# Splitting the first x loads into partition halves and the first gate steps into tiles, in an SSM and gated-MLP kernel

## The chip, the cores and the metric

The kernel runs on one core of one Trainium2 chip. The metric is device time in microseconds (us). Engines are TensorE (PE, with PEld for its weight loads), VectorE (DVE), ScalarE (ACT), GpSimd (POOL) and SyncE (SP); SP and ACT issue the DMA loads. A span is the profiled time from the first to the last instruction of an execution. For the kernel before, the time is about 1.8 us longer than the span.

## The reference

```python
def reference(A_x, Lambda.., B.., C.., log_dt, Dskip, B_x, w_gate, w_up, w_down):
    x  = A_x                                  # [1, 2048, 448] bf16
    xn = layernorm(x)
    # A: diagonal complex state space model along the sequence
    #    h_t = Lam_bar * h_{t-1} + B_bar xn_t ;  y = 2 Re(C h) + xn * Dskip
    s = A_ref(xn, ...)
    # B: gated MLP, 448 -> 1792 -> 448
    g = silu((sigmoid(xn @ w_gate) * (xn @ w_up)) @ w_down)
    return x + s * g
```

The 2048 tokens are 16 x tiles of 128 rows, worked on in four chunks of four tiles.

## The kernel before

The kernel records its operations with their costs, plans an order, and then emits them. Parts that the change touches, with cuts marked:

```python
    # head loads: x tiles 0, 1, and 2+3 together; gate weights wG in 3 blocks x 2 halves
    load_x(0, 1, "SP")
    load_w("SP", "g", 0, 0, rate=90e3)
    load_w("SP", "g", 0, 1)
    load_x(1, 1, "ACT")
    load_x(2, 2, "ACT")
    load_w("ACT", "g", 1, 0, rate=90e3)
    load_w("SP", "g", 0, 2)
    load_w("ACT", "g", 1, 1)
    load_w("ACT", "g", 1, 2)
    ...
    for h in range(2):
        load_w("SP", "u", h, 0, rate=215e3)
    load_x(4, 4, rate=300e3)                  # x tiles 4 to 7: chunk 1
    for h in range(2):
        load_w("SP", "u", h, 1, rate=215e3)
    ...
    def gu_mm(c, k, m, a, lo, hi, first):     # one gate or up step, token tiles lo..hi
        ts = slice(lo * P, hi * P)
        def f():
            for s in range(7):                # 7 pairs, each pair on the two halves of PE's rows
                T.matmul(gu[a][:, 0, ts], lhsT=w_[0:H, s, ms], rhs=x[0:H, s, ts], ...)
                T.matmul(gu[a][:, 1, ts], lhsT=w_[H:P, (s + 1) % 7, ms], rhs=x[H:P, s, ts], ...)
    ...
    # the head, in PE's order
    warm_mm(9); warm_mm(2, 128)               # 512 and 128 columns wide, on zeros
    stats(0); stats(1)                        # then normalise tiles 0, 1
    ...
    pe_transpose(0); pe_transpose(1)          # copies to xnT: tile 0 by ACT, the others by DVE
    ...
    warm_mm(2)
    gu_mm(0, "g", 0, slots0[0], 0, 2, True)   # 256 wide: tiles 0 and 1
    gu_mm(0, "g", 1, slots0[1], 0, 2, True)
    pe_transpose(2); pe_transpose(3)
    gu_mm(0, "g", 2, slots0[2], 0, 2, True)
    columns()
    for m in range(3):
        gu_mm(0, "g", m, slots0[m], 2, 4, False)
        gu_evac(0, "g", m, slots0[m])
    ...                                       # from here on steps of 512 columns
```

Of the kernel before, what the change touches and what calls it, by code (L numbers as in the profile page):

```python
# [14 lines left out]
ACT = mybir.ActivationFunctionType  # L15
# [3 lines left out]
D = 448  # L19
F = 1792  # L20
P = 128
H = 64
# [4 lines left out]
TPC = L // P  # L27
NTAB = L + 1
EPS = 1e-5
HEAD_DMA = 17  # L30
TWO_PI = 2.0 * math.pi
PI = math.pi
MAGIC = 12582912.0
# [40 lines left out]
class Plan:  # L74
# [10 lines left out]
    def add(self, eng, cost, fn, r=(), w=(), dma=0, lat=None, chain=False, name="", rate=230e3):  # L85
        o = Op()
        o.idx, o.eng, o.cost, o.fn, o.dma, o.name = len(self.ops), eng, cost, fn, dma, name
        o.lat = LAT.get(eng, 0.0) if lat is None else lat
        o.pre, o.suc, o.rate = {}, [], rate
        o.slot = None  # L90
        if dma and eng != "POOL":
            o.slot, self.n_dma = self.n_dma, self.n_dma + 1
        o.start = o.end = None
        for k in r:
            if k in self.w:
                self._edge(self.w[k], o, True)
        for k in w:
            for q in self.r.get(k, ()):
                self._edge(q, o, False)
            if k in self.w:  # L100
                self._edge(self.w[k], o, True)
        for k in w:
            self.w[k] = o
            self.r[k] = []
        for k in r:
            if k not in w:
                self.r.setdefault(k, []).append(o)
        if chain or eng == "PE" or (eng == "DVE" and self.seq):
            key = ("chain", eng)
            if key in self.last_of:  # L110
                self._edge(self.last_of[key], o, None)
            self.last_of[key] = o
        self.ops.append(o)
        return o
# [131 lines left out]
def kernel(  # L246
# [104 lines left out]
    def load(eng, key, nbytes, o, i, cost=0.45, r=(), rate=230e3):  # L351
        e = {"SP": Q, "ACT": A, "POOL": G}[eng]
        add(eng, cost, lambda: e.dma_start(out=o, in_=i), w=[key] if not isinstance(key, list) else key,
            r=r, dma=nbytes, chain=True, rate=rate)

    def load_x(t0, n, q="SP", r=(), rate=230e3):
        load(q, [("x", t) for t in range(t0, t0 + n)], n * P * D * 2,
             x_all[:, t0:t0 + n, :], x_src[:, t0:t0 + n, :], r=r, rate=rate)
# [3 lines left out]
    def load_w(eng, k, half, b, r=(), rate=105e3):  # L362
        m0, m1 = BLK[k][b]
        ps = slice(half * H, half * H + H)
        c0 = half * 896
        load(eng, [("w", k, half, m) for m in range(m0, m1)], H * 7 * (m1 - m0) * P * 2,
             wgt[k][ps, :, m0 * P:m1 * P],
             wsrc[k][:, c0 + m0 * P:c0 + m1 * P].rearrange("(s p) f -> p s f", p=H), cost=0.65, r=r, rate=rate)
# [24 lines left out]

    def load_p(eng, k, r=()):
        load(eng, ("vrow", k), D * 2, vrow[k:k + 1, :], (A_log_dt, A_Lambda_im, A_Lambda_re)[k].unsqueeze(0), cost=0.75, r=r)
    load_x(0, 1, "SP")
    load_w("SP", "g", 0, 0, rate=90e3)
    load_w("SP", "g", 0, 1)
    load_x(1, 1, "ACT")
    load_x(2, 2, "ACT")  # L400
    load_w("ACT", "g", 1, 0, rate=90e3)
    load_w("SP", "g", 0, 2)
    load_w("ACT", "g", 1, 1)
    load_w("ACT", "g", 1, 2)
    load_p("POOL", 0, [("wv", 0)])
    load_p("POOL", 1)
    load_p("POOL", 2)
# [88 lines left out]
    def pe_transpose(t):  # L496
        b, a, js = t % NXN, next_acc(), slice(t * P, t * P + P)
        tp = flat(acc[a][:].bitcast(BF16)[:, 0:7 * P], 7, P)

        def f():  # L500
            for s in range(6):
                T.transpose(tp[:, s, :], xn[b][:, s * H:s * H + P], ident[:, :])
            T.transpose(tp[0:H, 6, :], xn[b][:, 384:448], ident[:, :])
            T.transpose(tp[H:P, 6, :], xn[b][:, 0:H], ident[:, :])
        add("PE", 0.46, f, r=[("xn", b), "ident"], w=[("acc", a)])
        if t == 0:
            add("ACT", 0.85, lambda: A.copy(out=xnT[0][:, :, js], in_=tp[:, :, :]),
                r=[("acc", a)], w=[("xnT", 0, t, "a"), ("xnT", 0, t, "b")])
        else:
            add("DVE", 0.64, lambda: V.tensor_copy(out=xnT[0][:, :, js], in_=tp[:, :, :]),  # L510
                r=[("acc", a)], w=[("xnT", 0, t, "a"), ("xnT", 0, t, "b")])
# [8 lines left out]

    def xr(c, lo=0, hi=TPC):
        return [("xnT", c % 3, j, h) for j in range(lo, hi) for h in "ab"]

    def gate(keys, key):
        add("NONE", 0.0, lambda: None, w=list(keys) + (key if isinstance(key, list) else [key]), lat=0.0)

    def prepare(c):
        if c == 2:
# [409 lines left out]
        ssm_pair(c, 2)  # L938


    warm_mm(9)
    warm_mm(2, 128)
    pl.seq = True
    stats(0)
# [1 line left out]
    for t in (0, 1):  # L946
        chain(t, 1)
        norm(t)
    stats(2)
    slots0 = [next_gu() for _ in range(3)]  # L950
    pe_transpose(0)
    pe_transpose(1)
    stats(3)
    for t in (2, 3):
        chain(t, 1)
        norm(t)
    warm_mm(2)
    gu_mm(0, "g", 0, slots0[0], 0, 2, True)
    gu_mm(0, "g", 1, slots0[1], 0, 2, True)
    pe_transpose(2)  # L960
    pe_transpose(3)
    silu_table()
    pl.seq = False
    gu_mm(0, "g", 2, slots0[2], 0, 2, True)
    columns()
    for m in range(3):
        gu_mm(0, "g", m, slots0[m], 2, 4, False)
        gu_evac(0, "g", m, slots0[m])
    b_load()
    load_wd(0)  # L970
# [79 lines left out]
    a = next_acc()  # L1050
    yout(3, 3, banks=[(("acc", a), acc[a]), free_banks[4]], parts=((0, 128), (128, 448)))

    pl.solve({"g0.0": 5.9})
    with tc.manual_schedule():
        pl.emit()
    if globals().get("PLAN_HOOK"):
# [31 lines left out]
```

## Time and profile before

| | kernel before |
|---|---|
| time, median of 6 runs (range) | 187.17 us (186.67 to 187.88) |
| span of the profiled execution | 185.5 us |
| first gate matmul | 8.06 us |
| first 512-wide gate step | 14.38 us |
| first up step | 20.43 us |
| x tiles 4 to 7 landed | 17.60 us |

The prediction, below, shows the page, PE's head and the chain of waits. What it did not show, and what turns out to matter, is SP's own timeline (start, duration, engine, line, operation, tensors, count) and two rows of the page: what the DMA engines moved per slice of 4.64 us, and the queue that brings in instructions.

```profile
0.72 0.40 SPq L353 DMA_DIRECT2D x_all<-in_A_x_dram  x1
1.19 2.17 SPq L353 DMA_DIRECT2D wG<-in_B_w_gate_dram  x3
6.75 1.27 SPq L353 DMA_DIRECT2D wU<-in_B_w_up_dram  x2
8.07 0.62 SPq L353 DMA_DIRECT2D x_all<-in_A_x_dram  x1
```

An issue holds its queue: the whole tile 0 took 0.40 us, a gate block 0.60 to 0.73. From the page:

```profile
GB/s 159 257 221 225 176 175 210 80 269 178 120 4 46 82 71 4 0 0 4 0 51 78 73 26 0 4 25 24 0 25 4 25 25 4 25 0 76 51 78 25
q8 instruction: 11, 0.18, 0.4%
```

The last line reads as 11 transfers, 0.18 MB, 0.4% of the DMA engines. The trace gives each of the 11 as 16384 bytes, and later in the program one comes per about 256 weight loads and matmuls of PE.

### The profile page before, as it was taken

Reading aid. Unit: us, or ns where it says so; the run is one execution under the profiler, and the core shown is the slowest. Engines: PE = TensorE matmul, PEld = TensorE weight load, DVE = VectorE, ACT = ScalarE, POOL = GpSimd, SP = SyncE. Lnnn points to the kernel's source line nnn. Section 1 sums busy time; section 2 is a strip of 40 time slices with the busy share of each in tenths; the row PEclk is TensorE's granted clock in tenths of the full one; section 3 lists DMA queues with packets and bytes.
Section 4 is the critical chain, followed back from the end, with each engine's and each line's share of the span. In section 5 each row is a group of like instructions: output and inputs, shape, how many; then the busy total and the mean of one; then the engine's idle time right before and its main releaser. Section 6 shows DMA issues by size and latency. Waiting matters only on the chain.

```text
span 185.5 us, 3527 instructions
## 1 busy us (share of the span) xinstructions
PE 179.9 (97%) x1375; PEld 88.5 (48%) x1375; DVE 165.8 (89%) x295; ACT 93.1 (50%) x140; POOL 38.5 (21%) x93
## 2 busy tenths in 40 slices
PE   7999999999999999999999999999999999999991
PEld 2675444464445444444445444444445544455550
DVE  3731999999989899999999999899999999999763
ACT  3449995973899994225375422427223516211110
POOL 7125451940168937000012100000000000000000
PEclk9999999999999999999999999999999999999998
DMA  5999999499302330000023300000000000002120
GB/s 159 257 221 225 176 175 210 80 269 178 120 4 46 82 71 4 0 0 4 0 51 78 73 26 0 4 25 24 0 25 4 25 25 4 25 0 76 51 78 25
DMA packets 30257, 13.43 MB, mean 72 GB/s; under 512 B 19744, under 2 KB 30240, under 8 KB 30240
## 3 DMA queue, kind: packets, MB, share of 16 engines
q1 hardware_dynamic: 28336, 12.05, 31.1%
q10 hardware_dynamic: 1808, 1.15, 2.5%
q8 instruction: 11, 0.18, 0.4%
q14 instruction: 6, 0.05, 0.1%
q0 software_dynamic: 96, 0.00, 0.0%
HBM read 6.77 MB, written 1.84 MB: 46 GB/s over the span
## 4 chain that ended last, share of the span: by engine, by line
PE 68%; DVE 15%; DMA 8%; ACT 4%; issue 2%; SPq 1%; DVEq 0%
PE gu L709 29%; PE acc L892 15%; PE acc L917 11%; PE gu L892 6%; DMA x_all<-in_A_x_dram 5%; PE gu L777 5%; DVE hF L726 4%; DMA wG<-in_B_w_gate_dram 3%; DVE wv L831 2%; DVE hT L581 1%; DVE bst L425 1%; ACT ctmp L675 1%; DVE ta L824 1%; PE gu L780 1%; DVE tb L825 1%
## 5 line engine op out<-in xcount | busy, mean ns | idle before, releaser
L709 PE MATMUL gu<-xnT,wG 64*128 64x512 bf16 (+1 forms) x231 | 46.1, 344 | 0.3 <-DVE xnT L510 0.3
L710 PE MATMUL gu<-xnT,wG 64*128 64x512 bf16 (+1 forms) x231 | 46.1, 344 | 0.0
L709 PE MATMUL gu<-xnT,wU 64*128 64x512 bf16 x196 | 46.0, 376 | 0.0
L710 PE MATMUL gu<-xnT,wU 64*128 64x512 bf16 x196 | 46.0, 376 | 0.0
L723 ACT ACTIVATE sig<-gu 128x1024 f32<-128x1024 f32 x21 | 21.4, 1022 | 30.3 <-PE gu L710 27.9
L892 PE MATMUL acc<-wd,hF 128*128 128x448 bf16 x168 | 33.8, 353 | 0.0
L892 PEld LDWEIGHTS <-hF 128*128 128x128 bf16 x224 | 21.4, 98 | 21.1 <-issue 1.7
L709 PEld LDWEIGHTS <-wG 64*128 64x128 bf16 x231 | 21.3, 94 | 20.9 <-issue 1.9
L709 PEld LDWEIGHTS <-wU 64*128 64x128 bf16 x196 | 18.1, 94 | 23.4 <-issue 1.3
L726 DVE SCALAR_TENSOR_TENSOR hF<-sig,gu 128x1024 bf16<-128x1024 f32 x21 | 25.4, 1212 | 1.9 <-PE gu L710 1.6
L831 DVE TENSOR_TENSOR_SCAN wv<-c_r,st,z 128x512 bf16<-128x512 f32 x18 | 22.9, 1275 | 0.0
L917 PE MATMUL acc<-cT,hT 128*128 128x448 bf16 (+1 forms) x112 | 22.4, 344 | 0.0
L710 PEld LDWEIGHTS <-wG 64*128 64x128 bf16 x231 | 21.2, 94 | 0.0
L710 PEld LDWEIGHTS <-wU 64*128 64x128 bf16 x196 | 18.1, 94 | 0.0
L777 PE MATMUL gu<-xnT,bT 128*128 128x512 bf16 x72 | 16.9, 379 | 0.0
L917 PEld LDWEIGHTS <-hT 128*128 128x128 bf16 x119 | 11.3, 98 | 10.0 <-issue 0.4
L898 ACT ACTIVATE g_t<-acc 128x448 bf16<-128x448 f32 x12 | 6.5, 540 | 16.1 <-PE acc L892 13.0
L425 DVE BATCH_NORM_STATS2 bst<-x_all 128x6 f32<-128x448 bf16 x12 | 7.0, 612 | 7.4 <-DMA x_all<-in_A_x_dram 7.4
L788 ACT CAST bus<-gu 128x1024 bf16<-128x1024 f32 x12 | 12.0, 1005 | 2.3 <-PE gu L777 2.3
L478 POOL COPY xn<-xn 128x64 bf16<-128x64 bf16 x12 | 5.9, 488 | 29.1 <-ACT xn L475 28.8
L923 DVE TENSOR_TENSOR o_t<-acc,xd 128x448 bf16<-128x448 f32 (+1 forms) x16 | 9.5, 595 | 2.6 <-PE acc L917 2.4
L898 ACT ACTIVATE g_t<-gu 128x448 bf16<-128x448 f32 x4 | 2.2, 544 | 18.8 <-PE gu L892 18.8
(142 smaller groups left out, 261.8 us busy)
## 6 DMA issues: line engine op xcount, KB each, us to landing
out_dram<-o_t SPq DMA_DIRECT2D x15, 112.0 KB, 1.7
wd<-in_B_w_down_dram SPq DMA_DIRECT2D x2, 784.0 KB, 5.1
x_all<-in_A_x_dram SPq DMA_DIRECT2D x3, 448.0 KB, 4.7
wU<-in_B_w_up_dram SPq DMA_DIRECT2D x2, 448.0 KB, 11.5
wU<-in_B_w_up_dram SPq DMA_DIRECT2D x2, 336.0 KB, 7.3
wG<-in_B_w_gate_dram SPq DMA_DIRECT2D x2, 224.0 KB, 6.1
wG<-in_B_w_gate_dram ACTq DMA_DIRECT2D x2, 224.0 KB, 6.2
xnT<-xn SPq DMA_TRANSPOSE x24, 2.4
```

Source lines behind the costliest of these rows:

```text
L425: add("DVE", 0.6, lambda: V.bn_stats(out=bst[b][:], in_=x_all[:, t, :]), r=[("x", t)], w=[("bst", b)])
L709: T.matmul(gu[a][:, 0, ts], lhsT=w_[0:H, s, ms], rhs=x[0:H, s, ts], start=(s == 0), stop=(s == 6))
L710: T.matmul(gu[a][:, 1, ts], lhsT=w_[H:P, (s + 1) % 7, ms], rhs=x[H:P, s, ts], start=(s == 0), stop=(s == 6))
L723: add("ACT", act(1024), lambda: A.activation(th, gu[a][:], ACT.Tanh, scale=0.5), r=[("gu", a)], w=[tk])
L726: add("DVE", dve1(1024), lambda: V.scalar_tensor_tensor(out=ho, in0=th, scalar=1.0, in1=gu[a][:], op0=ALU.add, op1=ALU.mult), r=[("gu", a) ...
L777: T.matmul(gu[a][:, i, :], lhsT=bT[:, kt, i, pt * P:pt * P + P], rhs=x[:, 2 * kt, :], start=False, stop=(kt == 2))
L788: add("ACT", act(1024), lambda u=u, a=a: A.copy(out=bus[u][:], in_=gu[a][:]), r=[("gu", a)], w=[("bus", u)])
L831: dve(1.194, lambda k=k: V.tensor_tensor_scan(out=wv[:, k, :], data0=rb, data1=z[:, k, :], initial=(st[pt][:, k, :] if c else 0.0), op0=AL ...
L892: T.matmul(d, lhsT=hF[c % 2][:, m, h, js], rhs=wd[:, ft, :], start=(ft == 0), stop=(ft == FT - 1))
L898: add("ACT", act(448), lambda: A.activation(g_t[g][:], d, ACT.Silu, scale=0.5), r=[key, "silutab"], w=[("gt", g)])
L917: T.matmul(y, lhsT=hT[c % 2][:, hm, js], rhs=cT[:, cm, c0:c1], start=(i == 0), stop=(i == 6))
L923: add("DVE", dve1(n), lambda od=od, y=y, c0=c0, c1=c1: V.tensor_tensor(out=od, in0=y, in1=xq[:, c0:c1], op=ALU.add), r=[key, ("xd", q)], w ...
```

## The change

The intent is an earlier start of PE: x tiles 0 and 1 each come in as two halves of 64 partitions on both queues, ahead of all weights; the copies of tiles 0 and 3 are split between ACT and DVE; and the first gate steps go tile by tile, so that they need only tile 0 to begin. The core of the diff:

```diff
-HEAD_DMA = 17
+HEAD_DMA = 20
-    load_x(0, 1, "SP")
-    load_w("SP", "g", 0, 0, rate=90e3)
-    load_w("SP", "g", 0, 1)
-    load_x(1, 1, "ACT")
-    load_x(2, 2, "ACT")
-    load_w("ACT", "g", 1, 0, rate=90e3)
-    load_w("SP", "g", 0, 2)
-    load_w("ACT", "g", 1, 1)
-    load_w("ACT", "g", 1, 2)
+    for t in range(2):
+        for q, h in (("SP", slice(0, H)), ("ACT", slice(H, P))):
+            load(q, ("xh", t, q), H * D * 2, x_all[h, t, :], x_src[h, t, :], rate=150e3)
+        gate([("xh", t, "SP"), ("xh", t, "ACT")], ("x", t))
+    for t in (2, 3):
+        load_x(t, 1, "SP" if t % 2 == 0 else "ACT", rate=130e3)
+    for b in range(3):
+        load_w("SP", "g", 0, b, rate=130e3)
+        load_w("ACT", "g", 1, b, rate=130e3)
 ...
-        if t == 0:
-            add("ACT", 0.85, lambda: A.copy(out=xnT[0][:, :, js], in_=tp[:, :, :]), ...)
+        if t in (0, 3):
+            add("ACT", 0.46, lambda: A.copy(out=xnT[0][:, 0:3, js], in_=tp[:, 0:3, :]), ...)
+            add("DVE", 0.42, lambda: V.tensor_copy(out=xnT[0][:, 3:7, js], in_=tp[:, 3:7, :]), ...)
+        elif t == 1:
+            add("ACT", 0.9, lambda: A.copy(out=xnT[0][:, :, js], in_=tp[:, :, :]), ...)
 ...
-    warm_mm(9)
+    warm_mm(8)
 ...
-    warm_mm(2)
-    gu_mm(0, "g", 0, slots0[0], 0, 2, True)
-    gu_mm(0, "g", 1, slots0[1], 0, 2, True)
+    for j in range(2):
+        for m in range(2):
+            gu_mm(0, "g", m, slots0[m], j, j + 1, not (j or m))
+    gu_mm(0, "g", 2, slots0[2], 0, 1, False)
     pe_transpose(2)
+    gu_mm(0, "g", 2, slots0[2], 1, 2, True)
     pe_transpose(3)
 ...
-    gu_mm(0, "g", 2, slots0[2], 0, 2, True)
     columns()
+    for j in (2, 3):
+        for m in range(2):
+            gu_mm(0, "g", m, slots0[m], j, j + 1, not (j == 3 or m))
+    gu_mm(0, "g", 2, slots0[2], 2, 4, False)
     for m in range(3):
-        gu_mm(0, "g", m, slots0[m], 2, 4, False)
         gu_evac(0, "g", m, slots0[m])
```

More of the change, by code (lines that the diff above doesn't have):

```diff
@@ L354, in load, with gate @@
             r=r, dma=nbytes, chain=True, rate=rate)
+    def gate(keys, key):
+        add("NONE", 0.0, lambda: None, w=list(keys) + (key if isinstance(key, list) else [key]), lat=0.0)
     def load_x(t0, n, q="SP", r=(), rate=230e3):
@@ L505, in pe_transpose @@
         add("PE", 0.46, f, r=[("xn", b), "ident"], w=[("acc", a)])
-        if t == 0:
-            add("ACT", 0.85, lambda: A.copy(out=xnT[0][:, :, js], in_=tp[:, :, :]),
+        if t in (0, 3):
+            add("ACT", 0.46, lambda: A.copy(out=xnT[0][:, 0:3, js], in_=tp[:, 0:3, :]),
+                r=[("acc", a)], w=[("xnT", 0, t, "a")])
+            add("DVE", 0.42, lambda: V.tensor_copy(out=xnT[0][:, 3:7, js], in_=tp[:, 3:7, :]),
+                r=[("acc", a)], w=[("xnT", 0, t, "b")])
+        elif t == 1:
+            add("ACT", 0.9, lambda: A.copy(out=xnT[0][:, :, js], in_=tp[:, :, :]),
                 r=[("acc", a)], w=[("xnT", 0, t, "a"), ("xnT", 0, t, "b")])
@@ L522, in xr @@
         return [("xnT", c % 3, j, h) for j in range(lo, hi) for h in "ab"]
-    def gate(keys, key):
-        add("NONE", 0.0, lambda: None, w=list(keys) + (key if isinstance(key, list) else [key]), lat=0.0)
     def prepare(c):
@@ L948 @@
         norm(t)
-    stats(2)
     slots0 = [next_gu() for _ in range(3)]
@@ L952 @@
     pe_transpose(1)
+    stats(2)
     stats(3)
@@ L1051 @@
     yout(3, 3, banks=[(("acc", a), acc[a]), free_banks[4]], parts=((0, 128), (128, 448)))
-    pl.solve({"g0.0": 5.9})
+    pl.solve({"g0.0": 5.4})
     with tc.manual_schedule():
```

## The prediction

> **What bounds the kernel now.** I read the page first, then the chain of waits in order of time, then the engines' timelines of the first 20 us, then the chain around 54 us.
>
> The page says that TensorE (PE) is the bound over the whole:
>
> ```profile
> PE 179.9 (97%) x1375; PEld 88.5 (48%) x1375; DVE 165.8 (89%) x295; ACT 93.1 (50%) x140; POOL 38.5 (21%) x93
> DMA  5999999499302330000023300000000000002120
> ```
>
> PE has nothing to spare after its start, VectorE (DVE) is next at 89%, and DMA is saturated for the first ten slices of 4.64 us. The change touches only the first 14 us, so I split the span there. PE's timeline of the head:
>
> ```profile
> 5.43 0.82 PE L502 MATMUL acc<-ident,xn 128*128 128x128 bf16 x6
> ...
> 7.18 0.60 PE L419 MATMUL gu<-hF 128*128 128x512 bf16 x2
> ...
> 8.06 0.27 PE L709 MATMUL gu<-xnT,wG 64*128 64x256 bf16 x1 [0.28 <-DVE xnT L510]
> ```
>
> The first gate step starts at 8.06 us and waits for DVE's copy of tile 1's transpose. Everything before is warm-up or transposes, so up to about 1 us of PE time looks recoverable there. From 8.06 to 14.38 us (where the first 512-wide step starts) lie five 256-wide gate steps, two transposes, the column matmuls and one more gate step: 6.32 us.
>
> The chain of waits tells another story for what comes next:
>
> ```profile
> 8.07 9.54 DMA x_all<-in_A_x_dram
> 17.60 0.02 issue
> 17.63 0.64 DVE bst L425
> ```
>
> and, around 54 us,
>
> ```profile
> 52.49 0.68 ACT junk L432 x2
> 53.17 0.02 issue
> 53.19 0.67 ACT junk L432 x2
> 53.86 0.92 ACT sig L723
> 54.78 0.04 issue
> 54.82 0.27 PE gu L765
> ```
>
> The chain that ends last does not run through PE before 54.82 us. It starts at the landing of x tiles 4 to 7 at 17.60 us, goes through DVE almost without a gap, then through ScalarE (ACT) from 46.87 us on, and hands over to PE at 54.82. DVE's own timeline shows the same start:
>
> ```profile
> 12.19 0.18 DVE L548 COPY pv<-acc 128x12 f32<-128x12 f32 x1 [0.52 <-PE acc L544]
> 17.63 0.63 DVE L425 BATCH_NORM_STATS2 bst<-x_all 128x6 f32<-128x448 bf16 x1 [5.26 <-DMA x_all<-in_A_x_dram]
> ```
>
> DVE stands idle for 5.26 us, in program order behind statistics of a tile that has not landed. How much PE loses is in the starts of its matmuls: pairs of 512-wide steps start 0.216 us apart everywhere, but the last one before 54.82 started at 54.36, so this one is 0.46 - 0.22 = about 0.25 us late. Between 14.38 and 54.36 no spacing exceeds 0.31 us, the ordinary cost of a change of matmul shape. So **PE has about 0.25 us of hidden wait at 54.8 us, and that wait belongs to the landing at 17.60, not to PE's start at 8.06**. After 54.82 PE runs without a wait to the end.
>
> **What the Trainium skill says.**
> 1. "DMA: Bandwidth & Descriptors", section "Rules for kernel authors": two transfers to disjoint partition halves serialize on the same 16 engines, "Don't bother". Its section "Issuing engines are not separate DMA queues" says that issuing from several engines saves only issue time. The trace agrees: x tiles 0 and 1, on two queues, landed at 3.22 and 3.39 us, together rather than twice as fast, and traffic is 264 GB/s from 1.9 to 4 us, 261 from 4 to 8, 232 from 8 to 12, whatever the split. But order matters: tile 0 shared the engines with tile 1, which is needed 0.7 us later.
> 2. "TensorE: Matmul & The Clock Gate", section "Back-to-back issue gap": 134 cycles for 128 columns, 262 for 256; but it also gives about 81 ns per matmul at 128 columns with a weight load each. Here six 128-wide transposes with a load each take 0.51 us, of which 0.22 is the last one's latency: (0.51 - 0.22) / 5 = 58 ns. The trace sides with the 56 ns figure. Gate pairs of 256 columns start 109 ns apart (8.06, 8.17, 8.28).
> 3. The same page, section "Part 1: The HAM clock gate": half clock until a window of about 3.4 us was busy. Here the warm-up matmuls start 427 ns apart (half rate) until 5.43, and the two at 7.18 us start about 0.22 apart, so the switch falls near 6.7 us.
> 4. "TensorEngine Tiling (Array Packing)", section "Key Properties": changing the tiling mode drains PE. The last gate pair starts at 9.48 and the next transpose at 9.70, 0.22 against 0.11: about 0.1 us per change.
>
> **The change part by part.**
>
> x tiles 0 and 1 as halves, ahead of all else. Tile 0 no longer shares the engines with tile 1: its data packets were spread from 1.8 to 2.7 us and its completion to 3.22; alone it should land near 2.9. Gain 0.3 us (estimate). Tile 1 stays near 3.4, before DVE wants it (2.9 + 0.63 + 0.1). From landing to normalised tile took 3.22 to 5.38 = 2.16, so now 5.05. One warm-up matmul less (9 to 8, 0.427 each) ends the warm-up near 4.9, so PE can take the transpose: 5.05 to 6.1, tile 1's to about 6.95.
>
> Copy of tile 0 split between ACT (3 of 7 blocks) and DVE (4 of 7). The whole took 0.91 us on ACT, the like on DVE 0.62; the parts should be some 0.5 and 0.4. Tile 0 is ready near 6.75 instead of 7.45. The gate's first tile step then waits for PE's second transpose (6.95), not for the copy, so it could start at 7.05: 1.0 us earlier, and the two 0.22 us warm-up matmuls at 7.18 go.
>
> The weights. The gate step also needs block 0 of wG, both halves. Before they were issued at 1.19 and 1.69 and landed at 6.74 and 7.33. Now two or three 0.4 us x issues precede them on each queue, so both are issued near 1.95. From issue to first packet took 2.05 us, so packets start at 4.0, some 0.4 us after x is through. 448 KB at 260 GB/s is 1.75 us, plus the tail of 1 to 1.5 us that the slowest engine adds: 7.0 to 7.5. I take 7.3 as the start of the gate: **0.75 us earlier**.
>
> The block of gate steps. Ten 128-wide steps of 7 pairs at 56 ns = 3.92 us replace five 256-wide ones at 7 x 109 ns = 3.82: +0.1. Tile 2's and 3's transposes no longer stand together: two more changes of mode, +0.2. Block 6.6 instead of 6.32. New waits inside: tile 1's copy is all on ACT (0.91), ready near 8.0, about when two tile steps end; the third gate row needs block 1 of wG (landed 8.54 and 9.25 before, no earlier now), which may cost 0.2 to 0.3; tile 2's square root queues behind ACT's copy. Sum: 7.3 + 6.6 + 0.2 = 14.1 against 14.38. **PE is some 0.3 us ahead at 14 us.**
>
> What is that worth? By the schedule's order, DVE, ACT and POOL do the same work in nearly the same order afterwards (one or two neighbours swap). So PE meets the 54.8 us wait 0.3 us earlier and waits 0.3 us longer, unless the chain from x tiles 4 to 7 moves. Those are issued earlier now (their queue slot comes free with wG block 0, and SP no longer stands between 3.4 and 6.75 us), but stand behind the same bytes: 448 KB x, 1568 wG, 672 wU. Bandwidth sets their landing, not issue. The hole near 3.6 to 4.0 costs up to 0.4 us, the queue kept full saves some 0.2. So the landing stays at 17.6, give or take 0.5. With s the shift of that landing and 0.3 the gain of PE, the end moves by the later of s and -(0.25 + 0.3). For s = 0: 0. Allowing for the author's tuning and for a landing slightly early, I say 187.0.
>
> **The rivals.**
> A. The head's gain goes to the end (PE is 97% busy): 0.3 to 1.0 us, 186.1 to 186.8. For it: PE has no visible wait after 8.06. Against it: the late start at 54.82.
> B. The landing of x tiles 4 to 7 comes earlier, as SP issues them 1.3 us sooner and no engine starves: end -0.5, 186.5. For it: SP's stall to 6.75. Against it: traffic does not fall below 200 GB/s then.
> C. The landing comes later, through the hole or more small transfers: 187.5.
> D. PE stays at half clock one window longer, as less warm-up precedes the transposes: the gate runs at half rate for up to 3 us, +1 us or so, of which 0.25 to 0.5 is hidden: 187.8.
>
> **Range and chances.** 2% is 3.7 us. The largest gain that I can build (all of A) is 1 us, the largest loss (C with D) some 1.5. The three runs of before span 186.67 to 187.88, so a median is good to about 0.4. I predict 187.0 us, 8 in 10 between 186.3 and 187.8; within 2% 0.98, faster 0.01, slower 0.01.
>
> **What would show it.** Right: tile 0's statistics start near 2.9; first gate matmul near 7.3; 128-wide pairs 56 ns apart; first 512-wide gate step near 14.1; DVE's statistics of tile 4 still start near 17.6; PE's wait at the pass near 54.8 grows to about 0.5 us. Wrong: pairs at 80 ns or more (the block grows by 1.7 us); a late landing of wG; the clock still halved after 7 us; or tile 4's statistics well away from 17.6, after which the end should follow them.

## The result, and the profile after

The changed kernel takes 189.78 us (median of 6 runs, 189.12 to 190.55), against 187.17 for the kernel before. Ratios here are the mean time of one kernel's runs over that of the other's of the same rounds, so not quite the ratio of the medians: 1.0143, 95% interval 1.0109 to 1.0177. So the change is slower, by 1.4%: less than 2%, as predicted, but outside the predicted range. The profiled spans are 185.5 and 187.8 us. Executions over 1.5% slower than the fastest of the same kernel are left out of the means.

| us | before | after | predicted |
|---|---|---|---|
| first gate matmul | 8.06 | 7.72 (its partner 8.20) | 7.3 |
| first 512-wide gate step | 14.38 | 15.24 | 14.1 |
| first up step | 20.43 | 22.84 | |
| x tiles 4 to 7 landed | 17.60 | 18.77 | 17.6 |
| span | 185.5 | 187.8 | |

SP's timeline after:

```profile
0.72 1.84 SPq L353 DMA_DIRECT2D x_all<-in_A_x_dram  x3
2.62 2.24 SPq L353 DMA_DIRECT2D wG<-in_B_w_gate_dram  x3
7.70 1.27 SPq L353 DMA_DIRECT2D wU<-in_B_w_up_dram  x2
9.01 0.62 SPq L353 DMA_DIRECT2D x_all<-in_A_x_dram  x1
```

The three x issues take 1.84 us on SP. Single records: the first half of tile 0 takes 0.58 us to issue on SP and 0.59 on ACT, where the first whole tiles took 0.40 and 0.41 on the same queues; the halves of tile 1 take 0.58 and 0.84. Half the bytes cost more issue time, not less. The whole tiles 2 and 3 behind them take 0.58 and 0.60 as well (0.41 and 0.45 in e13 below, behind whole tiles); why is not shown. The gate weights are issued at 2.62 us (2.88 on ACT) instead of 1.19 (1.69), and everything behind them moves by about 1 us. The same page row as before:

```profile
GB/s 112 240 229 208 207 154 219 109 219 160 192 0 0 100 78 21 3 0 0 0 31 90 65 40 3 0 24 3 24 24 0 24 28 0 24 0 79 51 73 24
```

Summed over the first four slices (of 4.638 and 4.695 us), 862 x 4.638 = 4.00 MB before against 789 x 4.695 = 3.70 MB after: 0.3 MB behind, some 1.3 us at the 230 GB/s or so of slices two to four. DVE's timeline:

```profile
3.28 0.63 DVE L428 BATCH_NORM_STATS2 bst<-x_all 128x6 f32<-128x448 bf16 x1 [2.16 <-DMA x_all<-in_A_x_dram]
6.88 0.43 DVE L512 COPY xnT<-acc 128x512 bf16<-128x512 bf16 x1 [0.84 <-ACT xnT L510]
18.79 0.63 DVE L428 BATCH_NORM_STATS2 bst<-x_all 128x6 f32<-128x448 bf16 x1 [5.17 <-DMA x_all<-in_A_x_dram]
```

Tile 0's statistics start at 3.28 us, not earlier than before (3.24 there). The two parts of the tile 0 copy run one after the other: DVE waits 0.84 us for ACT's part. And tile 4's statistics come 1.2 us later than the 17.63 of before. PE's timeline, at the gate's start and later:

```profile
7.72 0.23 PE L714 MATMUL gu<-xnT,wG 64*128 64x128 bf16 x1 [0.78 <-DMA wG<-in_B_w_gate_dram]
8.20 0.23 PE L715 MATMUL gu<-xnT,wG 64*128 64x128 bf16 x1 [0.25 <-DMA wG<-in_B_w_gate_dram]
...
17.39 0.38 PE L714 MATMUL gu<-xnT,wG 64*128 64x512 bf16 x1
17.41 0.38 PE L715 MATMUL gu<-xnT,wG 64*128 64x512 bf16 x1
19.16 0.39 PE L714 MATMUL gu<-xnT,wG 64*128 64x512 bf16 x1 [1.37 <-issue]
```

The gate waits for its weights, not for x. And at 17.41 something happens that nothing in the prediction accounts for: in the middle of a 512-wide step whose pairs start 0.216 us apart, the next pair starts 1.75 us later. "issue" means that no wait on a semaphore shows. The chain of waits has it too:

```profile
17.57 0.20 PE gu L714
17.77 0.02 PE gu L715
17.79 1.37 issue
19.16 0.39 PE gu L714
...
30.60 1.22 DVE hF L731
...
57.23 0.27 PE gu L770
```

From the stop the chain stays on PE until 30.6 us, goes through DVE and ACT, and hands over to PE at 57.23 us, as it did at 54.82 before: 2.41 us later. In this trace it does not run through the landing of x tiles 4 to 7, late as that is: 57.23 - 18.77 = 38.5 us, where the path from the landing took 37.2 before (54.82 - 17.60).

The loss at the first up step is 22.84 - 20.43 = 2.41 us too: 0.86 us up to the first 512-wide step and 1.53 us of stop. So in this execution PE's own head, with the stop, carries the loss to the pass near 55 us.

What lies on the DMA queues just ahead of the stop, from 16.2 to 17.7 us (same columns as in the queue rows above):

```profile
q1 hardware_dynamic: 243, 0.24, 109.3%
q8 instruction: 1, 0.02, 5.7%
```

One block of PE's program, 16.27 to 17.65 us, amid saturated data queues. PE goes on 1.5 us after it landed. The Trainium skill, "Runtime: NRT & Kernel Launch", section "Instruction fetch mechanics", says that programs are refilled in 16 KiB blocks of 256 instructions over a DMA queue that the sequencer drives itself, and that crossing a block boundary is "mostly hidden". The blocks agree with the trace; in the head of this kernel the crossing isn't hidden.

### The profile page after: what moved, and what is told of

Read it like the earlier page. It is cut to its first block, busy times and chain, and to the rows that moved or that the text cites. A ratio compares the mean times of both kernels' runs of the same rounds, so it can differ in the third digit from the quotient of the medians.

```text
span 187.8 us, 3658 instructions
## 1 busy us (share of the span) xinstructions
PE 178.9 (95%) x1435; PEld 88.7 (47%) x1442; DVE 165.7 (88%) x295; ACT 94.1 (50%) x142; POOL 39.7 (21%) x93
## 3 DMA queue, kind: packets, MB, share of 16 engines
HBM read 6.77 MB, written 1.84 MB: 46 GB/s over the span
## 4 chain that ended last, share of the span: by engine, by line
PE 77%; DVE 10%; DMA 5%; ACT 4%; issue 2%; SPq 0%; DVEq 0%
PE gu L714 38%; PE acc L897 14%; PE acc L922 11%; PE gu L897 6%; PE gu L782 5%; DMA wG<-in_B_w_gate_dram 4%; DVE hF L731 2%; DVE wv L836 2%; DMA x_all<-in_A_x_dram 1%; ACT ctmp L680 1%; PE gu L785 1%; PE gu L715 1%; DVE ta L829 1%; DVE tb L830 1%; ACT bus L793 1%
## 5 line engine op out<-in xcount | busy, mean ns | idle before, releaser
L714 PE MATMUL gu<-xnT,wG 64*128 64x512 bf16 (+2 forms) x266 | 46.9, 320 | 2.1 <-issue 1.4
L715 PE MATMUL gu<-xnT,wG 64*128 64x512 bf16 (+2 forms) x266 | 46.7, 320 | 0.6 <-DMA wG<-in_B_w_gate_dram 0.6
L714 PEld LDWEIGHTS <-wG 64*128 64x128 bf16 x266 | 22.0, 94 | 22.3 <-issue 3.0
L715 PEld LDWEIGHTS <-wG 64*128 64x128 bf16 x266 | 21.9, 94 | 1.0 <-DMA wG<-in_B_w_gate_dram 0.9
L782 PE MATMUL gu<-xnT,bT 128*128 128x512 bf16 x65 | 15.3, 379 | 0.5 <-issue 0.2
L903 ACT ACTIVATE g_t<-acc 128x448 bf16<-128x448 f32 x12 | 6.4, 541 | 16.2 <-PE acc L897 13.1
```

The lines of the kernel that those rows point to most:

```text
L782: T.matmul(gu[a][:, i, :], lhsT=bT[:, kt, i, pt * P:pt * P + P], rhs=x[:, 2 * kt, :], start=False, stop=(kt == 2))
L903: add("ACT", act(448), lambda: A.activation(g_t[g][:], d, ACT.Silu, scale=0.5), r=[key, "silutab"], w=[("gt", g)])
```

## The experiments

Three theories stood at first. **R**: PE stops for a block of its program. **L**: the half loads make all loads later. **D**: the shorter warm-up makes the clock fall to half (in these traces for windows of 3.41 us, as from 8.60 to 12.01 us in e15). Two more came on the way: **X**, that the landing of x tiles 4 to 7 sets the end through DVE and ACT, as the prediction held; and **Q**, that SP's queue of transposing loads is a second chain with the same end near 55 us. In the expectations the stop is put at PE's "449th" record; counted over weight loads and matmuls alone by their starts it stands ahead of the 447th (in e4 the 446th). All ratios are to the kernel before.

| run | kernel | time us | ratio (95%) |
|---|---|---|---|
| e1 | change, 128-wide steps joined to 256 | 190.69 | 1.0164 (1.0121 to 1.0207) |
| e2 | change with the loads of before | 187.90 | 1.0040 (0.9998 to 1.0082) |
| e3 | before, six gate steps split | 191.21 | 1.0179 (1.0116 to 1.0243) |
| e4 | before, three gate steps split | 188.80 | 1.0075 (1.0023 to 1.0127) |
| e5 | before, x tiles 4 to 7 first | 187.79 | 1.0022 (0.9985 to 1.0059) |
| e6 | e1, x tiles 4 to 7 first | 190.57 | 1.0194 (1.0128 to 1.0261) |
| e7 | change, x tiles 4 to 7 first | 190.01 | 1.0138 (1.0102 to 1.0174) |
| e8 | e1 with whole x tiles | 189.14 | 1.0096 (1.0052 to 1.0141) |
| e9 | before, narrow warm-ups | 189.35 | 1.0157 (1.0104 to 1.0211) |
| e10 | before, half x tiles | 191.75 | 1.0235 (1.0209 to 1.0261) |
| e11 | e8, PE kept busy | 188.02 | 1.0052 (1.0026 to 1.0078) |
| e12 | e5, down weights by ACT | 190.30 | 1.0159 (1.0131 to 1.0188) |
| e13 | change with whole x tiles | 188.57 | 1.0043 (1.0006 to 1.0081) |
| e14 | e5, down weights last | 196.18 | 1.0462 (1.0420 to 1.0503) |
| e18 | e5, down weights earlier | 187.20 | 0.9984 (0.9961 to 1.0007) |
| e19 | e13, PE kept busy | 188.96 | 1.0090 (1.0063 to 1.0116) |

Times are medians of all runs of a label. e15 and e16 are the changed kernel and the kernel before.

### Is it the stop? e1, e3, e4

e1 joins the 128-wide steps again where they are emitted; plan and loads stay those of the change:

```diff
+            if c == 0 and k == "g" and hi - lo == 1 and (m, lo // 2) in JOIN:   # all five
+                if lo % 2 == 0:
+                    return
+                ts = slice(lo * P - P, hi * P)
```

> The changed kernel with its ten 128-wide gate steps joined into five 256-wide ones; loads and the order of every other engine as in the changed kernel. TensorE has 140 instructions fewer before its fourth gate row. Theory R (TensorE ran out of program: in the changed kernel it stops for 1.75 us after its 449th recorded instruction, in the middle of a gate row where nothing can be waited for, while a 16 KB block of its program is fetched behind the loads): the stop near 17.8 us is gone; what is left is the late loads, tile 4's statistics near 18.8 us instead of 17.6, so the end is 1.0 to 1.3 us over the kernel before: 188.3 us. Rival L (the late loads alone cause the loss): unchanged, 189.6 to 190.0. Rival W (the 128-wide steps themselves are slow): first 512-wide gate step earlier by over 0.5 us.

e3 and e4 do the opposite: the kernel before, with six or three of its 256-wide gate steps emitted as two of 128, and nothing else:

```diff
-            for s in range(7):
+            for ts in [slice(j * P, j * P + P) for j in range(lo, hi)] if (m, lo) in SPLIT else [...]:
+              for s in range(7):
```

> The kernel before, unchanged in every engine's order, in which six 256-wide gate steps are each issued as two 128-wide ones back to back: the same work and waits, 0.1 us more TensorE time, 168 TensorE instructions more. Theory R: TensorE comes to its 449th instruction near 14.6 us and stops until the block of program arrives, at 18 to 19.7 us: a stop of 3 to 5 us and the end as much later, 190 to 192 us. Without R (rivals L and others): 187.2 to 187.4 us.

> As the run with six split steps, but only three are split: 84 TensorE instructions more than the kernel before. Theory R: TensorE comes to its 449th instruction near 19.2 us, about when the block arrives: a stop of 0 to 0.6 us, of which 0.25 us is hidden by the wait near 54.8 us; 187.1 to 187.6 us. Without R: 187.2 us. With the six-step run it gives a dose and a response: a loss that grows by steps' cost alone would be half of the other run's.

e3 shows the stop, longer and earlier, in the timeline of PE:

```profile
14.16 0.38 PE L712 MATMUL gu<-xnT,wG 64*128 64x512 bf16 x1
17.03 0.39 PE L713 MATMUL gu<-xnT,wG 64*128 64x512 bf16 x1 [2.50 <-issue]
```

Its block landed at 15.45 us. The stop is 2.66 us, less than the 3 to 5 expected, and a window at half clock follows it (17.63 to 21.05 us), so e3's 1.79% is not the stop alone; its one execution with a full clock took 188.96 us. e4, with half as many extra instructions, stops for 0.32 us, at the record before; that execution took 187.12 us, as the kernel before, and the others of e4 were slower than expected (188.19 and more). So short matmuls ahead of the 447th bring the stop about, without any of the change's loads; R stands for the stop. But e1, which has no stop, is as slow as the change (190.69 us): R is not sufficient. In e1 the x tiles landed at 19.54 us, and the chain of waits leads from there to PE:

```profile
9.12 10.42 DMA x_all<-in_A_x_dram
...
56.76 0.27 PE gu L777
```

That is 37.2 us from landing to PE's late start, as before (17.60 to 54.82): X explains this profiled execution (span 187.3). The other three executions of e1 had spans of 188.6 to 188.8, which no trace here explains.

### Is it the loads? e2, e8, e13

e2 gives the change the loads of the kernel before, all of them; e8 is e1 with x tiles 0 and 1 loaded whole, and e13 is the change with the same edit:

```diff
+    whole = pl.ops[n0:]
+    whole[0].fn = lambda: Q.dma_start(out=x_all[:, 0, :], in_=x_src[:, 0, :])
+    whole[1].fn = lambda: A.dma_start(out=x_all[:, 1, :], in_=x_src[:, 1, :])
+    whole[3].fn = whole[4].fn = lambda: None
```

> The changed kernel with the head loads of the kernel before (whole x tiles, old order and queues); tile-wise gate steps kept, so TensorE has as many instructions as the changed kernel. Theory R: TensorE starts its gate near 7.4 us, comes to its 449th instruction near 17 us, stops there until the block of program is in, near 19 to 19.7 us; the kernel before was at the same point of its work at 16.75, so the end is 2.2 to 2.9 us late: 189.4 to 190.1 us, although all loads are as before. Rival L: as the kernel before or up to 0.3 us better, 186.9 to 187.3.

> The changed kernel with joined gate steps, and x tiles 0 and 1 loaded whole (tile 0 from SP, tile 1 from ACT) instead of as halves; all other loads in the changed kernel's order. One issue of 0.6 us less on each queue ahead of the weights: block 0 of wG is issued near 1.9 instead of 2.6 us and lands 0.5 to 0.7 earlier (7.1 and 7.6), x tiles 4 to 7 the same, near 18.9 instead of 19.5. If the halves are what delays the stream: the end 0.5 to 1 us better than joined steps with halves, 189.7 to 190.2. If the even order is to blame (x tiles 2 and 3 ahead of all weights): no better, 190.7.

> The change with x tiles 0 and 1 loaded whole (tile 0 by SyncE, tile 1 by ScalarE) and all else kept, the tile-wise gate steps too. Theory L+R (the half loads delay every later load by about 1 us; besides, PE's program block for its 449th instruction becomes usable some 9.3 us, from 8.5 to 10.5, after PE's 128th instruction, and PE stops if it gets there earlier): gate weights issued at 1.65 us and landed at 6.7 and 7.1 us, x tiles 4 to 7 at 17.5 to 17.9 us; PE passes its 128th instruction about 8.5 us, reaches the 449th at 16.5 to 17.2 us and stops there for 0.3 to 2 us; span about 186.5, time 188.0 to 188.7, so the half loads are worth 1.1 to 1.8 us of the 2.6. Rival (the tile-wise steps with their stop carry the loss alone): 189.5 or more.

e13 is the direct test: one part of the change undone, the tile-wise steps kept. Gate weights were issued at 1.63 and 1.67 us, x tiles 4 to 7 landed at 17.78, and the ratio fell from 1.0143 to 1.0043. So the half loads cost about 1.0% (from the two intervals, give or take 0.5, an estimate), or 1.9 of the 2.6 us. The kernel before took longer in e13's rounds (mean 187.75 us, against 187.16 in the change's); by the mean times of the change and e13 alone it is 189.84 - 188.55 = 1.3 us. The time is in the expected range.

How the halves cost it is less clear: the gate weights, issued 1.0 and 1.2 us earlier, landed only 0.2 and 0.4 us earlier (7.46 and 7.80). Over the first 18.55 us the DMA engines moved 215 GB/s before, 197 in the change and 211 in e13.

The expected stop did not show: e13's profiled execution had a window at half clock (8.23 to 11.65 us), reached its 447th record at 18.33 and went on at once, as its block had landed at 16.99. e2 ends at the same ratio, between its two expectations, with a stop of 0.46 us; its profiled execution had a window at half clock as well (7.98 to 11.39 us) and took 189.17 us, the three others 187.62 to 188.13. e8, whole tiles with joined steps and no stop, isn't better than e13, so joining gains nothing that these runs resolve.

### The half loads alone: e10

```diff
+    def halves01(e, h):
+        def f():
+            for t in range(2):
+                e.dma_start(out=x_all[h, t, :], in_=x_src[h, t, :])
+        return f
+    pl.ops[n0].fn, pl.ops[n0 + 3].fn = halves01(Q, slice(0, H)), halves01(A, slice(H, P))
```

> The kernel before with x tiles 0 and 1 each loaded as two partition halves on both queues, and nothing else: the issues of the first gate-weight blocks go from 1.19 and 1.69 us to about 1.9 and 2.4 us. Theory L (late loads): tile 0 lands no earlier than before (3.1 to 3.3 us), the first gate weights about 0.6 us later (7.3 and 7.9 us), x tiles 4 to 7 at 18.2 to 18.8 us instead of 17.6, PE's wait near 54.8 us grows from 0.25 to about 1 us, and the time is 0.5 to 1.2 us longer: 187.7 to 188.4, with no stop at the 449th instruction. Rival (the halves are free, all of the loss is the instruction blocks): 187.2, the x landing within 0.3 us of 17.6.

This was meant to isolate L in the kernel before, and was confounded. The chain of waits:

```profile
1.99 4.36 DMA wG<-in_B_w_gate_dram
6.37 0.60 ACTq L353
```

ACT's third gate issue stood from about 4.3 to 6.37 us until SP's first gate block had landed. Behind it in ACT's order was the square root of tile 0's statistics, so PE's first transpose came at 8.14 us, and two windows at half clock followed (7.44 to 14.26 us). x tiles 4 to 7 landed at 17.60 us, against the expectation. The run shows that one load more on each queue can cost over 4 us; it doesn't tell what the halves cost in the change. e13 does.

### Do stop and landing repeat? e15, e16

> The changed kernel again, for the spread of its trace. If the theory holds: x tiles 4 to 7 land at 18.3 to 19.5 us again, and PE stops at exactly its 449th weight load or matmul for 0.3 to 2.5 us, going on about 1.5 us after an instruction block landed. If the stop was an accident of one execution: none longer than 0.3 us between 14 and 24 us. Time 189.1 to 190.6.

> The kernel before again, for the spread of its trace. If the landing of x tiles 4 to 7 is set by the issues ahead of it: 17.4 to 17.9 us again, no stop in PE between 14 and 24 us, and PE's wait near 54.8 us under 0.5 us. If it varies by itself: up to 18.7 us as in e9, whose loads were those of before, and then with a longer wait. Time 186.7 to 188.0.

e16 (187.2 us) repeats its first trace: landing 17.01, first up step 20.32, wait near 54.7 us 0.24. e15 (189.62 us) repeats the landing (19.05) but not the stop. It has something else, here by stages (busy time per engine, then the granted clock of PE, DMA share and GB/s), first e15, then the changed kernel's first trace:

```profile
8.60:12.00 3.40, 3.40 (x69) 3.28 (x63) 1.55 (x6) 1.86 (x3) 0.37 (x2) 0.50 1.12 230
```

```profile
8.60:12.00 3.40, 3.07 (x85) 2.52 (x80) 1.60 (x6) 1.58 (x2) 0.18 (x1) 1.00 1.11 235
```

The second half of tile 0 landed at 3.84 us in e15, PE idled 1.15 us ahead of the transposes (0.49 in the first trace), and the clock was at 0.50 for one window: theory D. First 512-wide step 16.55 us, first up step 22.59, span 187.5. So two executions lose 2.2 and 2.4 us at the first up step in different ways. What they share is when PE passes its 447th record: 19.15 and 18.73 us. But a clock window does not go with a longer time over the change's six executions: the two with a mean clock of 0.991, as one window gives, took 189.75 and 189.40 us, the four others 189.12 to 190.55.

### Keeping PE busy: e11, e19

e11 is e8, and e19 is e13, with one more warm-up at the start and four or three after tile 1's transposes:

```diff
-            for _ in range(n):
+            for _ in range(n + (n == 8)):
 ...
+            if t == 1:
+                for _ in range(4):                                   # e19: 3
+                    T.matmul(gu[2][:, 0, :], lhsT=warm[:, 0:P], rhs=warm[:, 0:512], ...)
```

> The kernel of e8 (change with joined gate steps and whole x tiles) with PE kept busy by one more warm-up at the start and four after tile 1's transposes. Theory D (PE's pauses before the gate let the clock fall to half for one 3.41 us window in some executions): no execution shows a clock under 0.995, and the spans are all like those of e8's two undisturbed executions, 185.9 to 186.5 us, so about 0.5 us less than e8's mean; the rest, up to 0.5 us over before, is the wait near 55 us that hangs on SyncE's queue. Rival (the clock windows come by chance, whatever PE does): two of the six executions at 0.986 to 0.991 again, mean span 186.6.

> The kernel of e13 (the change with x tiles 0 and 1 whole, tile-wise steps kept) with PE kept busy by one more warm-up at the start and three after tile 1's transposes. Theory R as a floor (PE cannot pass its 449th weight load or matmul before some 1.5 us after its program block has landed, which is 8.5 to 10.5 us after PE's 128th): no window at half clock (no execution under 0.995), PE reaches its 449th early, at 16.3 to 17.2 us, stops there for 0.4 to 2 us and goes on at 17.5 to 18.6 us, so that up steps start at 21.3 to 22.3 us; span 185.8 to 186.5, time within 0.5 us of e13's 188.6 for all that PE starts on time. Rival (the half-clock windows are what is left of the loss): no stop, and the span falls to that of before, 185.5.

No execution of either has a clock under 0.995, where two of e8's four had 0.986 and 0.991, two of e13's six 0.987; the kernel before shows none under 0.995 in the rounds of the experiments. D is right as to the clock. In e11 the fast spans are 186.0 to 187.3 us, as expected but for that last one. In e19 the stop came back as a floor would have it, from the chain of waits:

```profile
17.56 0.02 PE gu L723
17.58 1.01 issue
18.59 0.39 PE gu L722
```

PE was at its 447th record at 17.4 us, early, and went on 1.44 us after its block had landed (17.15). But e19's spans (186.7 to 187.7 us, expected 185.8 to 186.5) are no better than e13's (186.2 to 187.2): the warm clock gains nothing at the end, and its trace has the stop in the window's place.

### What sets the stop: e9

```diff
-            for _ in range(n):
-                T.matmul(gu[2][:, 0, 0:w], lhsT=warm[:, 0:P], rhs=warm[:, 0:w], ...)
+            for _ in range({9: 64, 2: 14}[n] if w == 512 else n):
+                if w == 512:
+                    T.matmul(gu[2][0:32, 0, 0:64], lhsT=warm[:, 0:32], rhs=warm[:, 0:64], ...)
+                else: ...
```

> The kernel before with its 9 + 2 wide warm-up matmuls issued as 64 + 14 narrow ones (64 columns wide, 32 columns of weights): 134 more instruction rows on PE ahead of the gate, as many as the change adds, and nothing else touched; gate, loads and plan are those of before. Theory R (PE's program comes in blocks, and PE stops at its 449th weight load or matmul until a block has landed): before reaches that instruction at 23.9 us; 134 rows earlier is about 134 x 0.054 = 7.2 us earlier, at about 16.7 us; the block should land at 15.5 to 18.2 us, and PE goes on some 1.5 us after a landing, so PE stops at exactly its 449th record for 0.3 to 3 us, and the time is 0.3 to 2.8 us longer (187.5 to 190.0). Rival (the stop belongs to the tile-wise gate steps, their tile switches or their weights' late landing): no stop longer than 0.3 us between 14 and 24 us, time as before, 187.2.

R in the form "134 instructions more, hence a stop" failed: there is none. But the block came earlier as well, at 12.15 us where it came at 16.84 before, landed at 13.49, and PE reached the 447th record only at 15.75. The extra loss of e9 (1.57%) is not the stop: x tiles 4 to 7 landed at 18.72 us, for a reason that the trace doesn't show, and PE waited 1.04 us at 25.21 for DVE, which had started late.

So the number of instructions isn't the point; the time between two of them is. Over the traces (us; "goes on" is the start of the 447th record, in e4 of the 446th):

| run | PE's 128th record | block landed | goes on | goes on - landed | stop |
|---|---|---|---|---|---|
| before | 10.14 | 18.21 | 23.88 | 5.7 | none |
| change | 9.17 | 17.65 | 19.15 | 1.50 | 1.53 |
| change again (e15) | 10.04 | 17.09 | 18.73 | 1.64 | none |
| e2 | 9.61 | 17.36 | 18.88 | 1.52 | 0.46 |
| e3 | 8.21 | 15.45 | 17.03 | 1.58 | 2.66 |
| e4 | 9.55 | 17.72 | 19.15 | 1.43 | 0.32 |
| e7 | 10.22 | 18.19 | 19.65 | 1.46 | 1.08 |
| e9 | 4.41 | 13.49 | 15.75 | 2.3 | none |
| e13 | 9.33 | 16.99 | 18.33 | 1.34 | none |
| e19 | 9.23 | 17.15 | 18.59 | 1.44 | 1.17 |

Wherever PE stopped, it went on 1.43 to 1.58 us after the landing; e13 passed without a stop 1.34 us after its landing, so the lag varies a little. The block lands 7.1 to 9.1 us after PE's 128th record (over the runs, the time from a record to the block's start scatters least for a record between about the 120th and the 180th, so the request is likely made there; that is inferred). In the head, with the data queues saturated, 8.8 to 10.0 us so passed from the 128th record to going on, in the six traces with a stop. PE needs 13.7 us for the 319 records from the 128th to the 447th in the kernel before (23.88 - 10.14), but with 128-wide pairs at 56 ns only 6.2 us in e3 (14.37 - 8.21) and 8.5 us in the change (17.63 - 9.17): then it stops.

### The second chain near 55 us: e5, e6, e7, e12, e14, e18

e5, e6 and e7 issue x tiles 4 to 7 ahead of the up weights, in the kernel before, in e1 and in the change:

```diff
     for h in range(2):
         load_w("SP", "u", h, 0, rate=215e3)
     load_x(4, 4, rate=300e3)
+    p, q, r = pl.ops[n0:n0 + 3]
+    p.fn, q.fn, r.fn = r.fn, p.fn, q.fn
```

> The kernel before with one swap in SP's queue: x tiles 4 to 7 are issued ahead of the two first blocks of wU instead of behind them; every engine's order is unchanged. Theory X (the landing of x tiles 4 to 7 sets the chain that hands over to TensorE near 54.8 us): tile 4's statistics start near 15 us instead of 17.6, the 0.25 us wait near 54.8 us is gone, and the end is 0.2 to 0.3 us earlier: 186.9 us. The wU blocks land near 17.6 us, before 20.4 when they are wanted. Rival (that chain does not bind): 187.2 us.

> The changed kernel with joined gate steps (no stop for program) and with x tiles 4 to 7 issued ahead of wU. Theory X: what joined steps alone still lost (190.7 us) was the late landing of x tiles 4 to 7 (19.5 us in its trace); with the landing near 17 us only TensorE's late start is left: it reached the up steps at 21.12 us against 20.43, so 0.7 less 0.25 hidden, 187.7 us. Rival (the loss comes from TensorE's head itself, or from something not seen): it stays above 189.5 us.

> The changed kernel with x tiles 4 to 7 issued ahead of wU, nothing else. Its TensorE still stops after the 449th instruction. Theory R and X together (two separate losses of about the same size that run side by side): TensorE reached the up steps at 22.84 us against 20.43, so the end stays 2.0 to 2.4 us over the kernel before, 189.4 us, although the landing is early. If X alone is the cause: 187.7 us as with joined steps.

In e5 the tiles landed at 13.78 us instead of 17.60, and the time did not fall (187.79 us). PE's wait near 55 us grew to 1.7 us, and the chain of waits comes from elsewhere:

```profile
41.77 4.36 DMA xnT<-in_A_C_im_dram
46.22 0.68 ACT ctmp L678
46.91 0.70 DVE cT L681
...
54.63 0.92 ACT sig L726
55.59 0.27 PE gu L768
```

It is the load of C, and ahead of it SP's queue, where each transposing load takes 1.2 to 1.3 us or more to issue. So X as the only chain fell: the landing of x tiles 4 to 7 can come 3.8 us earlier and gain nothing. e6 and e7 show the same for the change: no gain. The profiled executions of both had a window at half clock across the gate (e6 7.49 to 10.90 us), and e7 the stop as well.

Three runs moved the two loads of the down weights (784 KB each) out of SP's way. e12 issues them from ACT:

```diff
+        pl.ops[-1].fn = lambda: A.dma_start(out=wd[:, fs, :], in_=...)
```

> The kernel of e5 (before with x tiles 4 to 7 issued ahead of the up weights) with the two loads of the down weights issued by ScalarE instead of SyncE. Theory Q (SyncE's queue, where every transposing load holds the queue for some 1.25 us, is a second chain that ends at PE's wait near 55 us): each of the two issues taken away saves 0.6 to 0.7 us on that chain, so PE's wait at 55.6 us falls from 1.7 us to about 0.5 us, and the span from 186.0 to about 185.0 us; time 186.3 to 187.0, which would be just under before. Rival (the chain is held by DMA bandwidth, or by ACT, not by the issues): the wait stays above 1.3 us and the time at 187.8.

e12 answered nothing: ACT issued the first of them at 17.44 us, ahead of B's loads, which then landed 4.5 to 7.4 us later than in e5, and PE waited 2.9 us at 31.13. (Its profile is slow; only the order of events is taken from it.) e14 issues the second one last, behind C and x tiles 8 to 15:

```diff
+    late = [o for o in pl.ops[n1:] if o.eng == "SP"]      # wd half 1, C x4, x 8-11, x 12-15
+    fns = [o.fn for o in late]
+    for o, fn in zip(late, fns[1:] + fns[:1]):
+        o.fn = fn
```

> The kernel of e5 (before with x tiles 4 to 7 issued ahead of the up weights) with the load of the second half of the down weights issued last on SyncE, behind the four loads of C and x tiles 8 to 15, which all move up by one place. Theory Q (SyncE's queue of transposing loads is a second chain, which holds PE near 55 us): the C loads are issued 0.63 us earlier and no longer share the DMA engines with 800 KB of down weights, so they land 1 to 2 us earlier than in e5 (before 45.5 us), PE's wait of 1.7 us near 55 us falls under 0.9 us, and the time is 186.3 to 187.2. Rival (that wait hangs on DVE's and ACT's own work, not on SyncE): the wait stays above 1.4 us and the time at 187.7.

That was a mistake about when PE needs these weights, as PE's timeline says:

```profile
48.91 0.91 PE L895 MATMUL acc<-wd,hF 128*128 128x448 bf16 x2 [6.07 <-DMA wd<-in_B_w_down_dram]
```

PE needs the second half in the middle of its first down projection, which had begun at 41.34; the clock then stood at half from 45.19 to 52.02 us. But the other half of the claim showed: with no down weights in front, the last load of C landed at 42.79 us, against 47.19 in e5. e18 puts the load earlier instead, ahead of the eight transposing loads of x tiles 4 to 7, by the same kind of rotation:

```diff
+    for o, fn in zip(early, fns[-1:] + fns[:-1]):
+        o.fn = fn
```

> The kernel of e5 (before with x tiles 4 to 7 issued ahead of the up weights) with the load of the second half of the down weights moved ahead of the eight transposing loads of x tiles 4 to 7, next to the first half (e14 had put it last, and PE, which needs it at 42.7 us, waited 6.2 us). Theory Q (PE's wait of 1.7 us near 55 us in e5 hangs on the landing of C, which shares the DMA engines with these weights and is issued behind them): C lands at 43 to 45.5 us (47.2 in e5), PE's wait near 55 us falls under 1 us, PE starts its down projection without a wait near 41.5 us, time 186.3 to 187.3, which would be at or just under before. Rival (the wait hangs on DVE's and ACT's own work): wait above 1.4 us, time 187.8.

C landed at 45.61 us, and PE starts that pass without a wait, 0.25 us after the pair ahead of it:

```profile
54.73 0.38 PE L765 MATMUL gu<-xnT,bT 64*128 64x512 bf16 x1
54.74 0.38 PE L766 MATMUL gu<-xnT,bT 64*128 64x512 bf16 x1
54.98 0.27 PE L768 MATMUL gu<-xnT,bT 64*128 64x256 bf16 x1
```

Q holds in these traces: the wait of 1.7 us went when C landed earlier. The time is 187.20 us against 187.45 in the same rounds, ratio 0.9984 with an interval that includes 1. It is the best kernel, and not shown to beat the kernel before.

## Why the prediction was wrong

**Within 2%: right. 187.0 us, range to 187.8: wrong by 2.8 us.** By its own steps:

- *Tile 0 alone lands near 2.9 us.* Wrong: its halves landed at 3.01 and 3.18 us (3.84 for the second in e15), and DVE started at 3.28. The prediction quoted the skill's "Don't bother" on halves and then expected 0.3 us from them all the same.
- *Copy parts of 0.5 and 0.4 us, tile 0 ready near 6.75.* The sizes are right (0.48 and 0.43); the sum is wrong, as DVE's part waited for ACT's: ready at 6.88 + 0.43 = 7.31 us. The Trainium skill, "PSUM — Partial Sum Buffer", section "PSUM bank collisions raise a hardware error", has it that no two engines may be in one bank and partition at once, so two copies out of one tile take turns; the trace agrees, with its wait of 0.84 us.
- *"Two or three 0.4 us x issues", gate weights issued near 1.95 us, landed by 7.0 to 7.5.* **This is the first step that failed on PE's path**, a mis-sized term: the x issues took 0.58 to 0.84 us each, not 0.4. The weights were issued at 2.62 and 2.88 us and landed at 7.68 and 8.16, so the gate's pairs began at 8.20 instead of 7.3. Undoing the half loads as a whole is worth 1.3 to 1.9 us (e13); that the issue time carries all of that is not shown.
- *The block of steps, 6.6 us; 512-wide steps from 14.1.* Pairs were 56 ns apart, as said. The next gate block landed at 10.22 us and cost a wait of 0.49, where 0.2 was counted. Measured 15.24, so PE was 0.86 us behind at this step instead of 0.3 ahead.
- *"Bandwidth sets their landing, not issue", 17.6 give or take 0.5.* Wrong: the DMA engines got their work later and were 0.3 MB behind at 18.7 us. Landings of 18.77 and 19.05 us in the change, 17.60 and 17.01 before. Rival C had the direction, and half the size. But in the change's trace the end does not hang on this landing.
- *The end moves by the later of the landing's shift and of PE's gain.* In the change's trace PE's shift set the end, but as a loss: 2.41 us at the first up step and again near 57 us (57.23 against 54.82). The wait of 0.25 us there hid none of it and did not grow to 0.5 either, as the chain through DVE and ACT came from PE itself by then. Besides, the term was incomplete, twice. e5 shows that another chain, through SP's queue and C, holds PE near 55 us. And **a term was missing altogether**: the block of PE's program, which PE, where it stopped, did not pass before 1.43 to 1.58 us after the landing. It took 1.53 us in the first trace of the change.
- *Rival D, the clock.* It happened in e15, not in the first trace; it was sized about right, but was held for a rival where it comes and goes from one execution to the next.

The parts do not add up. Late weights, the clock window and the program block all act ahead of PE's 447th record, and the block seems to be a floor under the other two (argued, from three traces): the change passes that record at 19.15 us with a stop and no window, at 18.73 with a window and no stop, and e19, which starts PE warm and on time, stops instead. **What is shown**: the half loads cost 0.7 to 1.0% (e13; e2, with all loads of before, agrees), the stop is a wait for a program block that short matmuls bring about (e3, e4, e19), and taking away the stop alone gains nothing as long as the loads are late (e1). **What stays open**: by which path the half loads cost that much; why e1's unprofiled executions are 1.3 us longer than its profiled one; why x tiles 4 to 7 landed at 18.72 us in e9; and how the last 0.4 to 0.9% divide among stop, clock and the wait near 55 us, as e8, e11, e13 and e19 don't order themselves by any one of them.

## What to carry to other kernels

Count the issue time of each load on its queue before splitting it: here half a tile took longer to issue than a whole one (0.58 us against 0.40), and the loads behind it were issued about 1 us later. Splitting a matmul for an earlier start also makes PE run through its program faster, which can end in a wait for the program itself; look for "issue" in the middle of a step and for the instruction queue's transfers. When a floor lies under several delays, removing one of them shows the next, so undo parts of a change singly and in pairs before naming a cause.

## What the Trainium skill lacked or had wrong

- "Runtime: NRT & Kernel Launch", section "Instruction fetch mechanics", calls the cost of crossing a 16 KiB boundary "mostly hidden". Here PE stood 0.32 to 2.66 us at a crossing in the head, in six traces, as the block landed 7.1 to 9.1 us after the 128th record and PE went on 1.43 to 1.58 us after that. No page says how long a refill takes while the data queues are saturated.
- "DMA: Bandwidth & Descriptors", section "Rules for kernel authors", is right that halves don't pay, but gives as the reason only that they share the engines. Here the issue time grew too: 0.58 to 0.84 us per half tile against 0.40 for the whole first tile.
